# Routing of the first expert: where the weight splits, the row pieces and the count update are issued

## The chip, the cores and the metric

One core of a Trainium2 chip. The metric is the device time of one execution in microseconds (us), lower is better. Engines by the profile's names: PE (TensorE, matrix multiply), PEld (its weight loads), DVE (VectorE), ACT (ScalarE), POOL (GpSimd), SP (SyncE, which issues most transfers).

## The reference, cut to what matters

Three blocks follow each other: block-causal attention (4 x 8 heads, 576 positions, 64 wide), a mixture of eight experts, and a bilinear layer. All tensors are float32. The routing of the middle block is a greedy one with capacities:

```python
logits = x @ w_gate                      # 2304 tokens, 8 experts
order = np.argsort(-logits.flatten())
for idx in order:                        # best (token, expert) pairs first
    tok, e = idx // E, idx % E
    if assigned[tok] >= 0 or counts[e] >= cap: continue      # cap = 288
    assigned[tok] = e; counts[e] += 1
for e in range(E):
    out[mask_e] = relu(x[mask_e] @ w1[e]) @ w2[e]
# then, on its rows: ((x @ w_a) * (x @ w_b)) @ w_out
```

## The kernel before, in words

**Stages.** `attention` leaves the 2304 output rows transposed in `xT` and the logits in `logits`. Then `moe` serves the eight experts in the order in which they fill up. For each expert o: `route(o)` finds which expert fills next and which 288 tokens it takes; `ffn(o)` computes both layers of that expert and the bilinear layer of its rows; `outs(o)` scatters the result. `route(o+1)` is interleaved into `ffn(o)`, so only `route(0)` runs with no matrix work beside it.

**Order of the work.** Every engine executes its own instructions in the order in which the Python code emits them (`manual_schedule`). The functions are generators: a `yield` is a place where the caller may emit something else. For `route(0)` the caller (L756) emits nothing between the yields, apart from `pump(3)` once the tokens are known (L757), so the engine queues hold exactly the order of the source.

**route(0).** `search` (L415) finds the threshold in six digits (`QUICK`: 4, 5, 6, 6, 6 and 5 bits). For each digit, DVE compares 18 columns of tokens with 2 to the bits thresholds (L432, tile `mk`); PE counts them with 18 small matmuls (L438); DVE compares the counts with the capacity (L441, `hit`); one matmul picks the digit (L444); DVE forms the next thresholds (L449 to L454). `members` (L465) then ranks the tokens with two prefix matmuls (L490, L491) and turns the ranks into row numbers with one-hot tiles (L511) and 18 matmuls (L515); three indirect transfers on POOL (L526) fetch the 288 rows, 96 each, from the DRAM tensor `xs`. `update` (L530) lowers the capacities and marks the tokens as taken; it holds one matmul of its own (L545). `xprep` (L559) scales the fetched rows (L564, tile `xo`), transposes them (L569) and splits them into a high and a low part (L571 `xh`, L572 `xl`).

**Two fillers are emitted inside route(0).** `xrows` (L355), called `xr`, writes the 18 pieces of 128 rows into `xs`: four PE transposes (L360), an ACT copy (L362), a small POOL copy (L363) and a transfer on SP (L364) for each piece. After the last piece it closes the pool of `xT` and allocates `wbh` and `wbl` in its place. `wsplit` (L370), called `ws`, splits the 24 pieces of the bilinear weights `wa` and `wb`: a load on SP two pieces ahead (L377), an ACT cast (L384, `wah`), a DVE subtraction (L385, `wal`). Its first call issues three loads, the next ones one each.

Three row pieces are emitted ahead of `route(0)`. Each digit then emits one weight split (L439) between the counting matmuls and `hit`, and 3, 3, 3, 3, 2 and 1 row pieces behind the matmul that picks the digit (L446). In `ffn(0)` the main loop emits one more split at every eighth step (L764). Each step of `ffn` holds three matmuls of 288 columns (L635 to L637).

**Expert weights.** `pump` (L601) keeps four loads (`raw`, L610 to L614) and up to six split pieces (`spl`: ACT cast L621, DVE subtraction L622) ahead of PE. `pump(3)` starts as soon as `members(0)` is through: four loads on SP and three splits. SP also reads the expert's number from memory (L485) before it can issue these loads.

Of the kernel before, what the change touches and what calls it, by code (L numbers as in the profile page):

```python
# [338 lines left out]
def moe(ctx, tc, k, xs, rows, room, logits, w1, w2, wa, wb, wor, out, idf):  # L339
# [3 lines left out]
    E,CAP,C,R,Q=k.E,k.CAP,k.C,k.R,k.Q; F=1024; DM=512; FF=1536; XW=DM+8  # L343
# [45 lines left out]
    def bc(a,n): return a[:,:,None].to_broadcast([128,a.shape[1],n])  # L389
    def bm(a,n): return a[:,None,:].to_broadcast([128,n,a.shape[1]])  # L390

    def wait(n):
        for _ in range(n): yield
# [3 lines left out]
    xr,ws=xrows(),wsplit()  # L397
# [17 lines left out]
    def search(DIG):  # L415


        ND=len(DIG)
        quick=DIG is k.QUICK
        mk=rt.tile([128,C,TM],BF,name="mk"); hit=rt.tile([TM,E],BF,name="hit"); th=rt.tile([128,TM],I32,name="th")  # L420
        dg=rt.tile([128,1],I32,name="dg"); dgf=rt.tile([128,1],F32,name="dgf")
        bmi=rt.tile([128,1],I32,name="bmi"); bmj=rt.tile([128,TM],I32,name="bmj")
        w=rt.tile([128,E],F32,name="w"); wd=rt.tile([128,E],F32,name="wd"); wm=rt.tile([128,1],F32,name="wm"); st['w']=w
        def prepare(i):

            if i: V.tensor_tensor(bmi,bmi,dg,op=ALU.bitwise_xor)
            if i+2<ND: V.scalar_tensor_tensor(bmj,pi,DIG[i+2][0],bmi.to_broadcast([128,TM]),op0=ALU.logical_shift_left,op1=ALU.bitwise_xor)
        for i,(sh,nb) in enumerate(DIG):
            T=1<<nb
            t=(th if i else th0)[:,0:T].bitcast(F32)  # L430
            for c,n in CUT[T]:
                V.tensor_tensor(mk[:,c:c+n,0:T],bc(m[:,c:c+n],T),t[:,None,:].to_broadcast([128,n,T]),op=ALU.is_ge)  # L432
                yield from wait(3)
            if i: prepare(i-1)
            yield from wait(4)
            p=ps.tile([128,512],F32,name="m",bufs=1)
            for c in range(C):
                nc.tensor.matmul(p[0:T,0:E],mk[:,c,0:T],ca[:,0,c,:],start=c==0,stop=c==C-1)  # L438
            if quick: next(ws)  # L439
            yield from wait(1)  # L440
            V.tensor_tensor(hit[0:T],p[0:T,0:E],kk[0:T],op=ALU.is_ge)  # L441
            yield from wait(3)
            p=ps.tile([128,512],F32,name="m",bufs=1)
            nc.tensor.matmul(p[:,0:E],pw[0:T,k.SH.index(sh),:],hit[0:T],start=True,stop=True)  # L444
            if quick:
                for _ in range((3,3,3,3,2,1)[i]): next(xr)  # L446
            yield from wait(3)
            if i<ND-1:
                V.tensor_reduce(dg,p[:,0:E],axis=AX.X,op=ALU.max)  # L449
                if i==0:  # L450
                    V.tensor_scalar(bmi,dg,28,None,op0=ALU.logical_shift_left)
                    flip(bmi,dg,bmi)
                    V.scalar_tensor_tensor(th,pi,DIG[1][0],bmi.to_broadcast([128,TM]),op0=ALU.logical_shift_left,op1=ALU.bitwise_xor)
                else: V.tensor_tensor(th,bmj,dg.to_broadcast([128,TM]),op=ALU.bitwise_xor)  # L454
            else:

                V.scalar_tensor_tensor(wd,e8,1.0/16,p[:,0:E],op0=ALU.mult,op1=ALU.add)
                V.tensor_reduce(dgf,p[:,0:E],axis=AX.X,op=ALU.max)
                V.tensor_reduce(wm,wd,axis=AX.X,op=ALU.max)
                V.tensor_scalar(dg,dgf,-1.0,None,op0=ALU.add)  # L460
                V.tensor_scalar(w,wd,wm,None,op0=ALU.is_equal)
                V.tensor_tensor(bmi,bmi,dg,op=ALU.bitwise_xor)
        st['v']=bmi.bitcast(F32)

    def members(o):  # L465

        w=st['w']
        eid=rt.tile([128,1],I32,name="eid",bufs=2)
        x=rt.tile([128,2,C,E],BF,name="x4"); cw=rt.tile([128,2,C],F32,name="cw"); bt=rt.tile([128,2,C],BF,name="bt")
        V.tensor_tensor(x,ca,w[:,None,None,:].to_broadcast([128,2,C,E]),op=ALU.mult)  # L470
        V.tensor_reduce(cw,x,axis=AX.X,op=ALU.add)
        we=rt.tile([128,E],F32,name="we"); ef=rt.tile([128,1],F32,name="ef")
        if o<E-1:
            v=st['v']
            g=rt.tile([128,C],F32,name="g")
            V.scalar_tensor_tensor(g,m,v,cw[:,0],op0=ALU.is_gt,op1=ALU.mult)
            V.scalar_tensor_tensor(bt[:,1],m,v,cw[:,0],op0=ALU.is_equal,op1=ALU.mult)
            V.tensor_tensor(bt[:,0],g,cw[:,1],op=ALU.add)
        else:
            V.memset(bt[:,1],0.0)  # L480
            V.tensor_tensor(bt[:,0],un,cw[:,1],op=ALU.add)
        V.tensor_tensor(we,w,e8,op=ALU.mult)
        V.tensor_reduce(ef,we,axis=AX.X,op=ALU.add)
        V.tensor_scalar(eid,ef,-1.0,float(E),op0=ALU.mult,op1=ALU.add)
        reg=nc.sync.value_load(eid[0:1,0:1],min_val=0,max_val=E-1)  # L485
        st['reg',o]=reg
        yield from wait(7 if o<E-1 else 20)
        b2=bt.rearrange("p a c -> p (a c)")
        p=ps.tile([128,512],F32,name="m",bufs=1)
        nc.tensor.matmul(p[:,0:2*C],ub,b2,start=True,stop=True)  # L490
        nc.tensor.matmul(p[:,2*C:4*C],ones,b2,start=True,stop=True)  # L491
        yield

        pf=rt.tile([128,2*C],F32,name="pf"); z=rt.tile([128,2,C],F32,name="z"); zz=rt.tile([128,C],F32,name="zz")
        V.tensor_tensor_scan(pf,onec,p[:,2*C:4*C],1.0,op0=ALU.mult,op1=ALU.add)
        V.tensor_tensor(pf,pf,p[:,0:2*C],op=ALU.add)
        V.tensor_tensor(z.rearrange("p a c -> p (a c)"),pf,b2,op=ALU.mult)
        V.scalar_tensor_tensor(zz,z[:,0],-1.0,z[:,1],op0=ALU.add,op1=ALU.add)
        st['z']=z
        q=rt.tile([128,C,Q+1],F32,name="q"); sb=rt.tile([128,C],BF,name="sb")  # L500
        oh=rt.tile([128,C,TM],BF,name="mk")[:,:,0:R]; tq=rt.tile([128,C,Q+1,2],BF,name="tq")
        s=rt.tile([128,C],F32,name="sl")
        V.tensor_tensor(q,bc(zz,Q+1),bm(q4,C),op=ALU.is_ge)
        V.scalar_tensor_tensor(s,q[:,:,1],-float(R),zz,op0=ALU.mult,op1=ALU.add)
        V.scalar_tensor_tensor(sb,q[:,:,2],-float(R),s,op0=ALU.mult,op1=ALU.add)
        V.tensor_tensor(tq,q[:,:,:,None].to_broadcast([128,C,Q+1,2]),tok[:,:,None,:].to_broadcast([128,C,Q+1,2]),op=ALU.mult)
        yield
        p=ps.tile([128,512],F32,name="m",bufs=1)
        h=C//2
        for c0 in (0,h):  # L510
            V.tensor_tensor(oh[:,c0:c0+h],bm(r96,h),bc(sb[:,c0:c0+h],R),op=ALU.is_equal)  # L511
            yield from wait(4)
        yield from wait(4)
        for c in range(C):
            nc.tensor.matmul(p[0:R,0:2*Q+2],oh[:,c,:],tq[:,c].rearrange("p q t -> p (q t)"),start=c==0,stop=c==C-1)  # L515
        yield

        ix=rt.tile([R,Q+1,2],F32,name="ixf"); li=rt.tile([R,Q+1],F32,name="li"); idx=rt.tile([R,Q],I32,name="idx",bufs=3)
        V.tensor_copy(ix,p[0:R,0:2*Q+2].rearrange("p (q t) -> p q t",t=2))
        V.scalar_tensor_tensor(li,ix[:,:,0],128.0,ix[:,:,1],op0=ALU.mult,op1=ALU.add)  # L520
        V.tensor_tensor(idx,li[:,0:Q],li[:,1:Q+1],op=ALU.subtract)
        st['idx',o]=idx
        for _ in xr: pass
        xg=wk.tile([R,Q,XW],F32,name="xo",bufs=1)
        for q_ in range(Q):
            nc.gpsimd.indirect_dma_start(out=xg[:,q_,:],out_offset=None,in_=xs,  # L526
                                         in_offset=bass.IndirectOffsetOnAxis(ap=idx[:,q_:q_+1],axis=0))
        st['xg',o]=xg
# [47 lines left out]
    def route(o):  # L576
        if o<E-1:
            if o:
                yield from choose()
                yield from wait(1)  # L580
            yield from search(k.FEW if o else k.QUICK)
        else: last()
        yield from members(o)
        st['ready']=o
        if o<E-1: yield from update(o)
        yield from wait(8)
        while st.get('hdone',-1)<o-1: yield
        yield from xprep(o)


    D1,D2=2,2
# [168 lines left out]
    for o in range(E):  # L760
        side=route(o+1) if o+1<E else iter(())
        for i,_ in enumerate(ffn(o)):
            tick()
            if ws and i%8==0:  # L764
                if next(ws,1)==1: ws=None
            if tail is not None and next(tail,1)==1: tail=None
            if i>=SIDE: next(side,None)
            pump()
        for _ in side: pass
        tail=outs(o)  # L770
# [85 lines left out]
```

## Time and profile before

| | |
|---|---|
| median of 3 runs | 1023.86 us (1021.78 to 1024.03) |
| the profiled execution | 1020.96 us |
| its span in the profile | 1019.2 us |
| PE busy | 955.7 us (94%) |
| DVE busy | 712.0 us (70%) |
| ACT busy | 440.1 us (43%) |
| POOL busy | 204.5 us (20%) |
| mean granted clock of PE | 0.969 of full speed |

The profiled execution took 1.8 us more than its span, which runs from the first to the last instruction. All positions in the trace are microseconds from the start of the span. In the timeline a row gives the start, the length, the engine, the source line, the operation, output and inputs with shapes, the number of merged instructions, and in brackets the idle time of the engine before it with what ended it. "SPq" is SP's issue of a transfer.

### The profile page before, as it was taken

How to read it: one execution, taken by the hardware profiler on the slowest of the kernel's cores; microseconds unless marked ns; L12 is line 12 of the kernel's file. 1: busy time of each engine (PE TensorE's matmuls, PEld its weight loads, DVE VectorE, ACT ScalarE, POOL GpSimd, SP SyncE). 2: the span in 40 equal slices, each digit the busy share in tenths (PEclk: the TensorE clock that was granted, in tenths of full speed). 3: DMA queues.
4: the chain of work that ended last, by engine and by line, in shares of the span. 5: the costliest groups of instructions: out<-in, count | busy, mean ns of one | idle time of the engine just before them, and what ended most of it. 6: DMA issues, size and time to landing. Idle time of an engine off the chain costs nothing.

```text
span 1019.2 us, 20479 instructions
## 1 busy us (share of the span) xinstructions
PE 955.7 (94%) x7741; PEld 894.9 (88%) x7741; DVE 712.0 (70%) x1627; ACT 440.1 (43%) x1108; POOL 204.5 (20%) x215
## 2 busy tenths in 40 slices
PE   6998999986489999999999999999999999999996
PEld 5776877764389999999999999999999999999996
DVE  6899899984677877677667667766766776535421
ACT  5775767753354335224422522442253235224321
POOL 8676566621100011002001100200110011101001
PEclk9999999997589999999999999999999999999998
DMA  6696777624665146115403520450253046215300
GB/s 140 186 244 180 211 213 218 182 95 161 204 195 162 43 118 188 32 43 165 110 22 98 178 63 24 136 158 22 80 159 90 12 118 188 66 52 158 84 12 24
DMA packets 134563, 123.14 MB, mean 121 GB/s; under 512 B 64320, under 2 KB 97088, under 8 KB 134464
## 3 DMA queue, kind: packets, MB, share of 16 engines
q1 hardware_dynamic: 131392, 112.32, 38.9%
q0 software_dynamic: 3072, 9.51, 2.9%
q8 instruction: 61, 1.00, 0.4%
q14 instruction: 38, 0.31, 0.1%
HBM read 102.85 MB, written 18.95 MB: 120 GB/s over the span
## 4 chain that ended last, share of the span: by engine, by line
PE 79%; DVE 9%; DMA 4%; ACT 3%; POOL 3%; issue 2%; SPq 0%; ACTq 0%; DVEq 0%; POOLq 0%
PE h L635 13%; PE h L636 12%; PE h L637 12%; PE acc L635 8%; PE acc L636 8%; PE acc L637 8%; PE tr L172 3%; PE pv L190 3%; PE s L149 3%; DMA xo<-xs,idx 2%; PE m L438 1%; PE pv L149 1%; DVE mx L150 1%; PE acc L360 1%; PE h L744 1%
## 5 line engine op out<-in xcount | busy, mean ns | idle before, releaser
L635 PE MATMUL acc<-th,spl 128*128 128x288 f32 x640 | 191.7, 300 | 0.2 <-ACT th L686 0.2
L636 PE MATMUL acc<-tl,spl 128*128 128x288 f32 x640 | 189.4, 296 | 0.3
L637 PE MATMUL acc<-th,spl 128*128 128x288 f32 x640 | 189.5, 296 | 0.0
L622 DVE TENSOR_TENSOR spl<-raw,spl 128x512 fp32r<-128x512 f32 x224 | 152.9, 689 | 26.5 <-ACT spl L621 20.4
L621 ACT CAST spl<-raw 128x512 fp32r<-128x512 f32 x224 | 137.3, 620 | 37.0 <-PE acc L637 27.7
L526 POOL DMA_INDIRECT xo<-xs,idx x24 | 25.4, 1060 | 496.1 <-DVE cg L535 445.5
L636 PEld LDWEIGHTS acc<-tl,spl 128*128 128x128 f32 x640 | 120.8, 189 | 1.1 <-DVE tl L687 1.1
L635 PEld LDWEIGHTS acc<-th,spl 128*128 128x128 f32 x640 | 120.6, 188 | 0.4 <-ACT th L686 0.4
L637 PEld LDWEIGHTS acc<-th,spl 128*128 128x128 f32 x640 | 120.5, 188 | 0.0
L686 ACT CAST th<-h 128x288 fp32r<-128x288 f32 x96 | 38.3, 399 | 182.6 <-DVE h L684 180.0
L635 PE MATMUL h<-y,wah 128*128 128x288 f32 x384 | 116.2, 303 | 0.0
L635 PE MATMUL h<-y,wbh 128*128 128x288 f32 x384 | 115.2, 300 | 0.0
L636 PE MATMUL h<-y,wbh 128*128 128x288 f32 x384 | 113.4, 295 | 0.0
L637 PE MATMUL h<-y,wal 128*128 128x288 f32 x384 | 113.2, 295 | 0.0
L636 PE MATMUL h<-y,wah 128*128 128x288 f32 x384 | 113.1, 295 | 0.0
L637 PE MATMUL h<-y,wbl 128*128 128x288 f32 x384 | 113.1, 294 | 0.0
L684 DVE TENSOR_TENSOR h<-h,ta 128x288 f32<-128x288 f32 x96 | 44.5, 464 | 90.0 <-PE h L637 87.9
L679 ACT COPY ta<-h 128x288 f32<-128x288 f32 x96 | 38.3, 399 | 157.6 <-PE h L637 156.7
L635 PE MATMUL h<-xh,spl 128*128 128x288 f32 x256 | 79.5, 311 | 4.0 <-ACT xh L571 4.0
L157 ACT ACTIVATE A<-s,mx 128x128 f32<-128x128 f32 (+7 forms) x128 | 64.0, 504 | 38.3 <-DVE mx L150 36.8
L636 PE MATMUL h<-xl,spl 128*128 128x288 f32 x256 | 76.8, 300 | 1.2 <-DVE xl L572 1.2
L637 PE MATMUL h<-xh,spl 128*128 128x288 f32 x256 | 76.5, 299 | 0.0
(213 smaller groups left out, 2189.1 us busy)
## 6 DMA issues: line engine op xcount, KB each, us to landing
raw<-in_moe_w_dram SPq DMA_DIRECT2D x128, 256.0 KB, 3.2
raw<-wo SPq DMA_DIRECT2D x96, 256.0 KB, 2.7
cw<-in_moe_w_a_dram SPq DMA_DIRECT2D x12, 512.0 KB, 3.9
cw<-in_moe_w_b_dram SPq DMA_DIRECT2D x12, 512.0 KB, 4.7
cw<-in_moe_w_out_dram SPq DMA_DIRECT2D x12, 512.0 KB
xs<-spl SPq DMA_DIRECT2D x18, 260.0 KB, 2.2
kr<-in_k_dram SPq DMA_DIRECT2D x32, 128.0 KB, 5.4
qr<-in_q_dram SPq DMA_DIRECT2D x32, 128.0 KB, 2.8
```

Source lines behind the costliest of these rows:

```text
L149: nc.tensor.matmul(o,ww[:,i,:],kk[:,c:c+w],start=s0,stop=s1)
L157: nc.scalar.activation(o,view,AF.Exp,bias=mx[:,i:i+1],accum_out=sm[:,i:i+1])
L172: nc.tensor.transpose(p[:,128*m:128*m+128],A[:,off[i]+j,:],idf)
L190: nc.tensor.matmul(p[64*h:64*h+64,c,a-cut[c]:e-cut[c]],vv[:,j,h,:],AT[:,h,o:o+e-a],start=(j==0), stop=(j==(2 if c==0 else 4)),skip_group_c ...
L621: nc.scalar.copy(t[:,0,:],src)
L622: V.tensor_tensor(t[:,1,:],src,t[:,0,:].bitcast(F32),op=ALU.subtract)
L635: nc.tensor.matmul(p,wh,xh,start=s0,stop=False)
L636: nc.tensor.matmul(p,wh,xl,start=False,stop=False)
L637: nc.tensor.matmul(p,wl,xh,start=False,stop=s1)
L679: nc.scalar.copy(t,pa[:,:CAP])
L684: V.tensor_tensor(g,g,t,op=ALU.mult)
L686: later(1,lambda: nc.scalar.copy(gh,g))
```

## The change

- The digits of the first search emit no weight split any more.
- Each of the six digits emits two row pieces, where it was 3, 3, 3, 3, 2 and 1. The three pieces that are left, and the end of `xrows`, are emitted in `members`, behind the prefix matmuls and ahead of the one-hot tiles.
- For the first expert `update` is emitted behind `xprep`, no longer between the indirect transfers and `xprep`. Two weight splits are emitted where it stood.
- In `ffn(0)` a weight split is emitted at every seventh step, where it was every eighth. So 22 of the 24 splits lie there, where it was 18.

```diff
             for c in range(C):
                 nc.tensor.matmul(p[0:T,0:E],mk[:,c,0:T],ca[:,0,c,:],start=c==0,stop=c==C-1)
-            if quick: next(ws)
             yield from wait(1)
             V.tensor_tensor(hit[0:T],p[0:T,0:E],kk[0:T],op=ALU.is_ge)
...
             if quick:
-                for _ in range((3,3,3,3,2,1)[i]): next(xr)
+                for _ in range(2): next(xr)
...
         nc.tensor.matmul(p[:,2*C:4*C],ones,b2,start=True,stop=True)
+        for _ in xr: pass
         yield
...
         st['idx',o]=idx
-        for _ in xr: pass
         xg=wk.tile([R,Q,XW],F32,name="xo",bufs=1)
...
         yield from members(o)
         st['ready']=o
-        if o<E-1: yield from update(o)
+        if 0<o<E-1: yield from update(o)
+        if o==0:
+            for _ in range(2): next(ws)
         yield from wait(8)
         while st.get('hdone',-1)<o-1: yield
         yield from xprep(o)
+        if o==0: yield from update(o)
...
             tick()
-            if ws and i%8==0:
+            if ws and i%7==0:
                 if next(ws,1)==1: ws=None
```

## Rows read from the trace of the kernel before

**Rows 1.** Busy time by stretch: from:to, length, engines' busy (instructions), PE clock, DMA share, GB/s

```profile
236.60:266.00 29.40, 17.70 (x172) 15.38 (x170) 15.02 (x44) 12.39 (x23) 3.05 (x13) 0.60 0.63 215
266.00:285.10 19.10, 6.16 (x38) 4.48 (x37) 13.37 (x48) 3.91 (x8) 3.28 (x3) 0.50 0.60 174
325.00:350.00 25.00, 23.51 (x218) 22.93 (x218) 19.64 (x43) 9.72 (x21) 0.00 (x0) 1.00 0.20 64
350.00:1019.00 669.00, 655.45 (x5381) 645.40 (x5380) 427.55 (x1027) 235.04 (x520) 54.20 (x69) 1.00 0.32 91
```

**Rows 2.** What DVE waited for, 236 to 286: us in total, times, longest

```profile
DVE wal L385 <- ACT wah L384: 12.5, 6, 5.0
```

**Rows 3.** Timeline of the search, DVE and PE

```profile
236.61 0.46 DVE L432 TENSOR_TENSOR mk<-mm,mth 128x288 bf16<-128x288 f32 x1
...
242.91 0.16 PE L444 MATMUL m<-hit,mpw 16*128 16x8 bf16 x1 [5.18 <-DVE hit L441]
...
244.27 0.76 DVE L432 TENSOR_TENSOR mk<-mm,th 128x576 bf16<-128x576 f32 x1
...
247.93 1.68 PE L360 MATMUL acc<-idf,xT 128*128 128x128 f32 x12
...
256.75 0.16 PE L444 MATMUL m<-hit,mpw 64*128 64x8 bf16 x1 [1.06 <-DVE hit L441]
...
256.85 2.82 PE L360 MATMUL acc<-idf,xT 128*128 128x128 f32 x12
...
257.48 1.43 DVE L432 TENSOR_TENSOR mk<-mm,th 128x768 bf16<-128x768 f32 x2
...
259.60 1.12 PE L438 MATMUL m<-mca,mk 128*64 128x8 bf16 x18
...
261.88 1.97 PE L360 MATMUL acc<-idf,xT 128*128 128x128 f32 x8
...
263.78 0.65 PE L438 MATMUL m<-mca,mk 128*32 128x8 bf16 x18
...
265.96 0.16 PE L444 MATMUL m<-hit,mpw 32*128 32x8 bf16 x1 [1.54 <-DVE hit L441]
```

**Rows 4.** Timeline from the ranks to the fetched rows

```profile
270.07 1.58 SPq L610 DMA_DIRECT2D raw<-in_moe_w_dram  x3
...
271.48 1.86 PE L515 MATMUL m<-tq,mk 128*96 128x8 bf16 x18 [2.93 <-DVE mk L511]
...
273.01 0.62 ACT L621 CAST spl<-raw 128x512 fp32r<-128x512 f32 x1 [5.09 <-DMA raw<-in_moe_w_dram]
...
274.21 1.20 POOL L526 DMA_INDIRECT xo<-xs,idx  x1 [16.98 <-DVE g L534]
...
275.15 0.62 ACT L621 CAST spl<-raw 128x512 fp32r<-128x512 f32 x1 [0.63 <-DMA raw<-in_moe_w_dram]
...
277.19 0.92 POOL L526 DMA_INDIRECT xo<-xs,idx  x1 [0.30 <-issue]
...
282.91 0.69 DVE L564 TENSOR_TENSOR xo<-xo 96x512 f32<-96x512 f32 x1 [2.10 <-DMA xo<-xs,idx]
```

**Rows 5.** Line L364, the row writes: time from issue to landing

```profile
DMA to landing us min/median/max: 2.1/2.2/2.3
```

**Rows 6.** Line L526, all eight experts' fetches: time from issue to landing

```profile
DMA to landing us min/median/max: 4.6/4.8/5.7
```

**Rows 7.** The page's group of the expert weights' subtractions

```profile
L622 DVE TENSOR_TENSOR spl<-raw,spl 128x512 fp32r<-128x512 f32 x224 | 152.9, 689 | 26.5 <-ACT spl L621 20.4
```

**Rows 8.** Timeline: the update's head, and the first matmuls of ffn(0)

```profile
274.10 0.31 DVE L535 TENSOR_TENSOR cg<-mca,g 128x144 bf16<-128x144 bf16 x1
...
274.47 0.30 PE L545 MATMUL m<-cg,mones 128*128 128x144 bf16 x1 [1.13 <-DVE cg L535]
...
285.10 0.56 DVE L572 TENSOR_TENSOR xl<-h,xh 128x384 fp32r<-128x384 f32 x1 [0.57 <-ACT xh L571]
...
285.71 0.61 PE L636 MATMUL h<-xl,spl 128*128 128x288 f32 x1
```

## The prediction, made before the changed kernel was run

> **What bounds the kernel now.** I cut the span into stages first. From 350 us on PE is busy 655 of 669 us, so PE sets the pace and work on other engines is nearly free. The search (236.6 to 266.0) and the fetch of the rows (266.0 to 285.1) are different: PE is busy 17.7 of 29.4 us and 6.2 of 19.1 us, and the granted clock is 0.60 and 0.50 [rows 1]. These 48.5 us are a chain of dependent steps with no matrix work beside it. Whatever is taken off that chain comes off the end, since all later PE work stands behind it.
>
> Then I asked what the chain waits for. In it DVE waited 12.5 us, six times, for the ACT cast of a weight split, at the subtraction L385 [rows 2]. That subtraction is queued ahead of `hit`, the answer that every digit needs. So each of the six digits ends by its split, not by its counting. The longest wait, 5.0 us, is the first one, where the weights still had to be loaded.
>
> **Part 1, the search without splits.** I rebuild each digit from its rows. A digit starts with the matmul L444 that picks the digit before. In the trace the digit before the last starts at 256.75; its 12 transposes run 256.85 to 259.67, its comparison `mk` 257.48 to 258.91, its 18 counting matmuls start at 259.60 and take 1.12; but the next L444 comes only with the last digit, whose first transposes are at 261.88, so near 261.79 [rows 3]. Counting was through at 260.72; the missing microsecond is the split.
>
> Without the split the end is: counting, then 0.04 to `hit`, then 0.20 (`hit` itself and the step to PE) to the next L444; both small steps are estimates. With two pieces there are eight transposes, 1.97 at 261.88 where it was 2.82 for twelve [rows 3]. At this low clock:
> - First digit: `mk` ends at 237.07, 18 counts take 0.65 (as at 263.78), so L444 comes at 237.97 where it was 242.91. Saved 4.94.
> - Second digit: `mk` (244.27 + 0.76) ends 2.12 after its L444 at 242.91; plus 0.05, 0.61 for counts, 0.04 and 0.20 it lasts 3.02.
> - Three digits of 64 thresholds: the eight transposes end 2.0 after L444, counts start at about 1.95, plus 1.12, 0.04 and 0.20: 3.31 each.
> - Last digit: transposes end at 2.0, counts 0.65, so 2.88.
>
> The last L444 comes at 237.97 + 3.02 + 3 x 3.31 + 2.88 = 253.80 where it was 265.96 [rows 3]. **Saved: 12.16 us.** At the full clock (twelve transposes in 1.68 at 247.93 [rows 3]) the comparisons would be last: 3.10 three times and 2.42, so 252.7 and 13.25 saved. [...] Below this the rows give nothing.
>
> **Part 2, three pieces beside the one-hot tiles.** I keep the old positions here. PE stands idle 2.93 us ahead of the one-hot matmuls at 271.48, thus from 268.55 [rows 4]. Twelve transposes take 2.82 [rows 3]: they just fit, cost 0, and would cost up to that 0.1 to 0.3 if they began late. The last copy on ACT then ends near 272.0 and its row write lands 2.2 later [rows 5], at 274.25. The first fetch started at 274.21 [rows 4] and must wait for all rows: 0.05, between 0 and 0.5.
>
> **Part 3, splits and loads ahead of the fetch.** SP used to issue the expert weights' loads at 270.07. Now three row writes and four loads of the two splits stand ahead of them on SP, so the first load of that burst goes out at about 272.4. Unloaded, the first of three landed 2.94 after its issue (cast at 273.01) and the third 2.14 later (275.15): 1.07 each [rows 4]. The third expert piece is the seventh of the new burst: 272.4 + 2.94 + 6 x 1.07 = 281.8. Its cast takes 0.62 [rows 4], its subtraction 0.69 [rows 7], and all three scalings of the fetched rows (0.69 each) stand behind it on DVE: they end near 285.3. Before, the last scaling ended at 283.60, held by the third fetch [rows 4]. Cost 1.7, and 0.4 because the three transposes then come at once: 2.1, for the burst is nearest to the three loads of before. The bounds are 0 (the fetch stays last) and 3.3 (a pitch a fifth longer, as the fetch shares the engines). The two splits' own DVE and ACT work hides in the wait for the loads.
>
> The fetch's third transfer took 5.7 us, where the median over all experts is 4.8 [rows 6], beside four loads on SP. [...]
>
> **Part 4, `update` behind `xprep`.** Where it stood, DVE was waiting for the fetch anyway, so removing it gains 0 (it gave cover, not time). Where it goes, its matmul L545 stands in PE's queue ahead of the first matmul of `ffn(0)` and waits for `cg`. The last subtraction `xl` ends at 285.66; then a small operation of about 0.23 and `cg` of 0.31, then L545 of 0.30 [rows 8]. The second matmul of `ffn(0)`, which needs `xl`, used to start at 285.71 [rows 8]; it now follows L545 and the first one, at about 286.7, but no longer with a gap behind it. Cost 0.8, between 0.4 and 1.4. The rest of the update, some 2 us on DVE, delays the next expert splits, of which three are in hand, 36 matmuls or over 4 us of PE work (218 took under 25 us [rows 1]): 0.
>
> **Part 5, 22 splits in `ffn(0)`.** Four more subtractions are 2.8 us of DVE. Between 325 and 350 DVE is busy 19.6 of 25 us and PE still 23.5 [rows 1]; what PE misses there, 1.5 us, can grow with a busier DVE. I take 0.5, between 0 and 2.8 (all of it exposed). All splits are still issued before the columns that need them: the last at step 147, needed from step 156.
>
> **Sum.** -12.2 + 0.05 + 2.1 + 0.8 + 0.5 = -8.8, with a little for a partly full clock: **-9.0 us**. On the profiled execution (1020.96, span 1019.2) this gives 1012.0. The median of the runs is 2.9 above that execution, so on the median: 1023.86 - 9.0 = **1014.9**.
>
> **Rivals.**
> *The search runs at the full clock.* For it: without waits for the split PE is busy about 3.0 of each 3.3 us. Against it: the clock stayed at 0.50 to 0.60 here with PE more than half busy [rows 1]. Price: 1.1 more saved, and the last pieces land earlier, which takes 1 to 1.5 off Part 3: -11.5, thus 1012.4. [...]
> *The burst holds the fetch itself.* Last row writes, eight loads and the fetch meet; the fetch itself lands 4 us late and Part 3 costs 6 instead of 2.1: saved only 5, thus 1019. For it: 5.7 against 4.8 [rows 6]. [...]
> *The row pieces pace the search, not the splits.* Then DVE's wait would pass to PE's transposes, and nothing much is saved: 1023. Against it: at 256.75 counting was through 1 us ahead of `hit` even with twelve transposes [rows 3].
> [...]
>
> **How the numbers follow.** About 0.2% (2 us) is what a measurement of this kernel can tell from no change. Chances: the forecast 0.66, full clock 0.15, burst 0.12, row pieces 0.04, slower 0.03. The range takes in the first three: the low end is the full clock with Parts 4 and 5 at their least, -13, thus 1011.0; the high end has Part 3 at 3.3, Part 4 at 1.4 and Part 5 at 2.0: -5.4, thus 1018.5. Faster 0.94, no change 0.03, slower 0.03.
>
> **What would show it.** The waits of DVE should no longer have L385 behind ACT in the search; the first L444 should stand near 238.0 and the last near 253.8. Ahead of the last scaling DVE should wait for an expert load, not for the fetch, and L545 should stand directly ahead of the first matmul of `ffn(0)`, whose second one should start near 276.6 where it was 285.71. From there to the end the length should be that of before, within 1 us. I am wrong if a digit still lasts over 4 us, if the fetch's last transfer takes over 7 us, or if PE idles more than 3 us in `ffn(0)`.

## The result, and the profile after

The changed kernel took 1013.26 us (median of 5 runs, 1010.71 to 1014.97), the kernel before 1023.86 beside it: a ratio of 0.990, 95% interval 0.9878 to 0.9921, so 8 to 12.5 us less. The forecast was 1014.9, 9.0 less. The profiled execution of the changed kernel took 1013.26 us, its span 1011.5.

Busy time by stretch, columns as in [rows 1]: the search, from its first comparison to the last matmul that picks a digit, and the way from there to the first matmul of `ffn(0)`.

```profile
235.45:252.88 17.43, 14.54 (x156) 12.39 (x154) 11.37 (x38) 6.76 (x13) 4.62 (x13) 0.62 0.46 171
252.88:274.73 21.85, 7.62 (x54) 6.54 (x54) 13.97 (x41) 8.53 (x16) 3.47 (x3) 0.58 0.84 257
```

The search is 11.9 us shorter (29.35 before, from 236.61 to 265.96 [rows 3]). The stretch behind it is 2.7 us longer (19.16 before, 265.96 to 285.12), and PE's clock in the search is hardly higher. What DVE waited for from 236 to 277 (us, times, longest) shows what took the place of [rows 2]:

```profile
DVE hit L440 <- PE m L438: 4.2, 6, 1.1
DVE spl L624 <- ACT spl L623: 2.8, 3, 2.1
DVE wal L385 <- ACT wah L384: 2.6, 2, 2.4
...
DVE xo L563 <- DMA xo<-xs,idx: 0.7, 1, 0.7
```

Each `hit` now waits for the counting, and for nothing else. The timeline of the search answers to [rows 3]; two of the digits stand for all:

```profile
235.45 0.46 DVE L432 TENSOR_TENSOR mk<-mm,mth 128x288 bf16<-128x288 f32 x1
...
236.88 0.16 PE L443 MATMUL m<-hit,mpw 16*128 16x8 bf16 x1 [0.32 <-DVE hit L440]
...
246.63 0.16 PE L443 MATMUL m<-hit,mpw 64*128 64x8 bf16 x1 [0.25 <-DVE hit L440]
246.72 1.97 PE L360 MATMUL acc<-idf,xT 128*128 128x128 f32 x8
...
248.62 1.12 PE L438 MATMUL m<-mca,mk 128*64 128x8 bf16 x18
...
249.78 0.16 DVE L440 TENSOR_TENSOR hit<-m,mkk 64x8 bf16<-64x8 f32 x1 [0.60 <-PE m L438]
250.00 0.16 PE L443 MATMUL m<-hit,mpw 64*128 64x8 bf16 x1 [0.25 <-DVE hit L440]
...
252.88 0.16 PE L443 MATMUL m<-hit,mpw 32*128 32x8 bf16 x1 [0.24 <-DVE hit L440]
```

A digit of 64 thresholds lasts 3.37 us (246.63 to 250.00): eight transposes, then the counts, then `hit`. From the row numbers to the first matmuls of `ffn(0)`, answering to [rows 4, 8], the timeline reads:

```profile
258.93 2.08 SPq L377 DMA_DIRECT2D wraw<-wa  x4
...
260.36 0.16 DVE L521 TENSOR_TENSOR idx<-li 96x3 int32<-96x3 f32 x1
...
262.47 1.13 POOL L525 DMA_INDIRECT xo<-xs,idx  x1 [10.55 <-DMA wraw<-wa]
...
268.75 0.69 DVE L624 TENSOR_TENSOR spl<-raw,spl 128x512 fp32r<-128x512 f32 x1 [0.45 <-ACT spl L623]
...
270.11 1.96 DVE L563 TENSOR_TENSOR xo<-xo 96x512 f32<-96x512 f32 x3 [0.67 <-DMA xo<-xs,idx]
...
274.69 0.30 PE L544 MATMUL m<-cg,mones 128*128 128x144 bf16 x1 [1.65 <-DVE cg L534]
...
275.12 0.44 PE L638 MATMUL h<-xl,spl 128*128 128x288 f32 x1
```

The fetch starts 1.95 us behind the row numbers (260.52 to 262.47); in the kernel before it was 0.29. DVE is through with the third expert piece at 269.44 and then still waits 0.67 for the fetched rows. The update's matmul stands ahead of `ffn(0)` as forecast.

The last difference lies in `ffn(0)`. From its second matmul (285.71 before [rows 8], 275.12 after) to the first scatter transpose it takes 94.7 us before and 97.2 after. The start of that transpose is the first of the two positions in these groups of the scatter's line (min/median/max ns, first and last start), before and after:

```profile
L744 PE MATMUL h<-idf,y x96: 270/272/316, 380.4 to 1010.5; 128*96 128x128 f32 x96
```

```profile
L746 PE MATMUL h<-idf,y x96: 270/272/312, 372.3 to 1002.8; 128*96 128x128 f32 x96
```

Below, "search" is the first stretch, "scalings" the end of the third scaling counted from the end of `idx`, and "`ffn(0)`" this last length. For one execution each:

| | search | fetch starts | scalings | `ffn(0)` | ratio to the kernel before (95%) |
|---|---|---|---|---|---|
| before | 29.35 | 0.29 | 9.68 | 94.7 | 1 |
| changed | 17.43 | 1.95 | 11.55 | 97.2 | 0.990 (0.9878 to 0.9921) |
| a1, splits back | 27.02 | 1.71 | 11.24 | 94.8 | 1.0001 (0.9980 to 1.0022) |
| a2, pieces back | 15.28 | 0.29 | 8.83 | 96.4 | 0.9877 (0.9854 to 0.9900) |
| a3, update back | 16.60 | 1.71 | 15.29 | 96.9 | 0.9950 (0.9928 to 0.9972) |
| a4, splits behind the rows | 16.62 | 1.70 | 10.54 | 95.5 | 0.9922 (0.9893 to 0.9951) |
| b1, more transposes | 15.27 | 1.42 | 10.55 | 96.8 | 0.9886 (0.9859 to 0.9913) |
| b2, pieces back, update in the fetch | 15.28 | 0.30 | 8.28 | 97.2 | 0.9877 (0.9849 to 0.9905) |
| b3, pieces back, other steps | 15.27 | 0.29 | 8.74 | 97.4 | 0.9895 (0.9869 to 0.9921) |
| b4, b2 and b3 | 15.27 | 0.29 | 8.24 | 96.3 | 0.9874 (0.9843 to 0.9904) |
| c1, the change again | 17.18 | 1.71 | 12.13 | 96.2 | 0.9915 (0.9894 to 0.9936) |
| c2, subtractions on POOL | 17.42 | 1.96 | 11.74 | 97.9 | 0.9933 (0.9913 to 0.9952) |
| c3, b2 and c2 | 15.29 | 0.29 | 8.44 | 98.0 | 0.9876 (0.9856 to 0.9897) |
| d1, four splits early | 15.27 | 0.29 | 14.50 | 95.2 | 0.9912 (0.9880 to 0.9944) |

The attention ahead of all this is the same code everywhere, and yet the search began between 233.8 and 242.0 us in these executions. Whole times are therefore only good to some 3 us; the lengths in the table are what the experiments are read by.

### The profile page after: what moved, and what is told of

Read it like the earlier page. It is cut to its first block, busy times and chain, and to the rows that moved or that the text cites. A ratio compares the mean times of both kernels' runs of the same rounds, so it can differ in the third digit from the quotient of the medians.

```text
span 1011.5 us, 20472 instructions
## 1 busy us (share of the span) xinstructions
PE 954.3 (94%) x7741; PEld 893.9 (88%) x7741; DVE 711.2 (70%) x1627; ACT 439.9 (43%) x1108; POOL 206.4 (20%) x215
## 4 chain that ended last, share of the span: by engine, by line
PE 80%; DVE 10%; DMA 5%; ACT 2%; issue 2%; POOL 1%; SPq 0%; POOLq 0%; DVEq 0%; ACTq 0%
PE h L637 13%; PE h L638 12%; PE h L639 12%; PE acc L638 8%; PE acc L637 8%; PE acc L639 8%; PE tr L172 4%; PE s L149 3%; PE pv L190 3%; DMA xo<-xs,idx 3%; PE m L438 2%; DVE mx L150 1%; PE pv L149 1%; PE h L746 1%; DVE cf L801 1%
## 5 line engine op out<-in xcount | busy, mean ns | idle before, releaser
L624 DVE TENSOR_TENSOR spl<-raw,spl 128x512 fp32r<-128x512 f32 x224 | 153.0, 689 | 29.3 <-ACT spl L623 23.3
L686 DVE TENSOR_TENSOR h<-h,ta 128x288 f32<-128x288 f32 x96 | 44.4, 463 | 87.9 <-PE h L639 85.9
```

The source lines that it names most:

```text
L624: V.tensor_tensor(t[:,1,:],src,t[:,0,:].bitcast(F32),op=ALU.subtract)
L686: V.tensor_tensor(g,g,t,op=ALU.mult)
```

## The experiments

**a1: the splits back in the digits.**

```diff
+            if quick: next(ws)
             yield from wait(1)
...
-        if o==0:
-            for _ in range(2): next(ws)
...
-            if ws and i%7==0:
+            if ws and i%8==0:
```

> The changed kernel with the splits back in the six digits (one each), none beside the fetch, and every eighth step in ffn(0); the pieces stay two per digit, update stays behind xprep. If the splits paced the search: each digit ends by a split again, the search (first comparison to last digit-picking matmul, 17.4 us in the changed kernel, 29.4 before) comes back to about 27, a little under before because only two copies stand ahead of the cast; the fetch starts 0.3 us behind the row numbers again, and time is about 1013.3 + 9.8 - 1.9 (fetch) - 2 (ffn(0)) = 1019. If the row pieces paced it: the search stays under 20 us and time stays within 2 us of 1013.3.

Measured: a search of 27.02 us and the time of the kernel before. The splits were the cause; pieces and update alone win nothing. One part of the expectation failed: the fetch still started 1.71 us late, with no split's load near it (a4 shows why). DVE's waits show the splits again:

```profile
DVE wal L385 <- ACT wah L384: 10.2, 6, 5.1
```

**a2: the row pieces back in the digits.**

```diff
-                for _ in range(2): next(xr)
+                for _ in range((3,3,3,3,2,1)[i]): next(xr)
...
-        for _ in xr: pass
         yield
...
         st['idx',o]=idx
+        for _ in xr: pass
```

> The changed kernel with the pieces as before (3, 3, 3, 3, 2, 1 per digit, none beside the one-hot tiles). If the transposes end last in a digit at the low clock: the search grows by 0.85 us in each of three digits and 0.75 in the second, from 17.4 to 20.7. If the late row writes held the fetch (it started 1.95 us behind the row numbers, 0.29 before): it starts 0.3 us behind them again and ends 1.9 earlier, so 1013.3 + 3.3 - 1.9 = 1014.7. If the loads of the two splits held it by themselves: it still starts over 1.5 us late and time is about 1016.6.

Measured: the opposite of the first part. With half as many transposes again in a digit, the search is 2.15 us shorter than the changed kernel's, because PE ran it at the full clock, a granted 1.00 where it was 0.62. Its row by stretch, clock in the third column from the end:

```profile
236.66:251.94 15.28, 12.10 (x172) 10.26 (x170) 11.38 (x38) 8.41 (x17) 4.08 (x13) 1.00 0.71 264
```

Its digits of 64 thresholds take 2.81 us. The second part came: with the rows written early the fetch starts 0.29 behind `idx`, although the loads of the two splits are still there.

**b1: more work for PE, and nothing else.** In the changed kernel, four transposes of the identity behind the two pieces of each digit:

```diff
                 for _ in range(2): next(xr)
+                pj=ps.tile([128,512],F32,name="acc",bufs=4)
+                for g in range(4): nc.tensor.transpose(pj[:,128*g:128*g+128],idf,idf)
```

> The changed kernel with four more PE transposes per digit behind the two pieces, of the identity into a bank that nobody reads, so twelve per digit as with three pieces. If PE's clock decides the digit (the changed kernel had a granted clock of 0.62 in its search and 3.36 us per 64-threshold digit, the run with three pieces 1.00 and 2.81): the clock stays at 1.00, the digits take 2.81 and the search 15.3 us where it was 17.4; time falls by about 2. If the number of transposes decides: the clock stays low, digits take 4.2 and the search about 20. If it was the extra copies or row writes of three pieces: nothing changes, 17.4 or a little more.

Measured: a search of 15.27 us, with the same two copies and two row writes per digit as the changed kernel.

```profile
234.67:249.94 15.27, 12.47 (x175) 10.68 (x174) 11.37 (x38) 6.37 (x13) 4.60 (x13) 1.00 0.52 194
```

So the clock made the difference between eight and twelve transposes, not the rows. All seven kernels with twelve transposes in most digits and no split there had a granted clock of 1.00 in the search and took 15.3 us. Twelve alone are not enough: the kernel before had them too, in digits of 3.9 to 5.0 us, at 0.60 [rows 1]. With eight, the same search code ran at 0.62 in the changed kernel and at 0.77 and 0.76 in a3 and a4, where it took 16.6 us.

**a4: the two early splits behind the fetched rows.**

```diff
-        if o==0:
-            for _ in range(2): next(ws)
         yield from wait(8)
         while st.get('hdone',-1)<o-1: yield
         yield from xprep(o)
-        if o==0: yield from update(o)
+        if o==0:
+            for _ in range(2): next(ws)
+            yield from update(o)
```

> The changed kernel with its two early splits, and their four loads, emitted behind xprep instead of ahead of the fetch. If those loads held the last row write and the fetch: it starts at most 0.8 us behind the row numbers, its transfers land in 4.8 to 5.7 us (7.6, 6.7 and 5.7 in the changed kernel), and time falls by 1.5 to 2 to about 1011.5. If the last row writes are late by themselves, or any load behind them does the same: the fetch still starts over 1.5 us late, and time stays at 1013.3.

Measured: the fetch still starts 1.70 us late, but its transfers land in 5.3 us, where they took 5.7 to 7.6 in the changed kernel, and the scalings end 1.0 earlier. So the loads of the splits slowed the transfers, and did not hold the start. What does is seen in POOL's records of its waits (ns min/median/max, first and last start), of the kernel before, of the changed one and of a4:

```profile
L526 POOLq EVENT_SEMAPHORE  x6: 17/43/83627, 270.1 to 282.9; - x6
```

```profile
L525 POOLq EVENT_SEMAPHORE  x6: 17/43/86234, 261.3 to 271.4; - x6
L525 POOL DMA_INDIRECT xo<-xs,idx x3: 921/1134/1412, 262.5 to 265.6; - x3
```

```profile
L525 POOLq EVENT_SEMAPHORE  x6: 17/43/86724, 266.8 to 276.1; - x6
L525 POOL DMA_INDIRECT xo<-xs,idx x3: 921/1070/1137, 268.0 to 270.8; - x3
```

The first record marks the end of the wait for the last row write; the longest, of 84 to 87 us, is the last one, which waits for the next expert. In the changed kernel the last row write is issued at 258.48 and lands 2.8 us later, at 261.3, and the first transfer starts 1.1 us behind that (262.5). It is the same 1.1 in a4 (266.8 and 268.0) and in b1 (258.2 and 259.3). In the kernel before the wait was over at 270.1, long before `idx` was ready at 273.92, and only 0.29 was left. What the 1.1 us consist of, these runs do not show.

**a3: update back in the fetch.**

```diff
-        if 0<o<E-1: yield from update(o)
+        if o<E-1: yield from update(o)
...
-        if o==0: yield from update(o)
```

> The changed kernel with update back between the fetch and xprep, two splits behind it. If its move cost what its place in PE's queue says: the second matmul of ffn(0) starts 0.05 us behind the last subtraction xl again (0.98 in the changed kernel), and time falls by 0.8 to about 1012.5. If DVE's 2.6 us of update ahead of the fetched rows delay the scalings: the gain is used up or more, 1013.3 or above.

Measured: slower than the change, scalings at 15.29 us. But this is not the price of update. Its `yield`s let `pump` issue three more loads ahead of the splits' loads on SP:

```profile
259.06 1.58 SPq L611 DMA_DIRECT2D raw<-in_moe_w_dram  x3
260.84 0.36 SPq L615 DMA_DIRECT2D raw<-in_moe_w_dram  x1
263.53 0.37 SPq L611 DMA_DIRECT2D raw<-in_moe_w_dram  x1
265.04 0.34 SPq L615 DMA_DIRECT2D raw<-in_moe_w_dram  x1
266.14 0.37 SPq L611 DMA_DIRECT2D raw<-in_moe_w_dram  x1
266.56 6.73 SPq L377 DMA_DIRECT2D wraw<-wa  x5
```

Each of the three waits for a buffer (DVE is through with the three pieces ahead at 263.50, 265.01 and 266.11), and the splits' loads (258.93 in the changed kernel) stand behind them at 266.56. DVE then waits for the split, with the scalings behind it. The run tells nothing on update; b2 asks again.

**b2: update whole, right behind the transfers, with the pieces of a2.**

```diff
         if o==0:
+            for _ in update(o): pass
             for _ in range(2): next(ws)
...
-        if o==0: yield from update(o)
```

> The run with three pieces per digit, and update emitted whole right behind the indirect transfers, ahead of the two splits (the run with update back had the splits' loads behind loads that wait for free buffers, and its scalings ended 15.3 us behind the row numbers). If update costs only by its place in PE's queue: the scalings end about 8.8 us behind the row numbers as with three pieces alone, the second matmul of ffn(0) starts 0.05 to 0.1 behind the last xl instead of 0.98, and 0.8 is saved against three pieces alone: 0.9870 of the kernel before. If DVE has no room for it in the fetch: the scalings end over 9.6 behind the row numbers and nothing is saved.

Measured: scalings at 8.28 us, not later than in a2, and the second matmul of `ffn(0)` follows `xl` again:

```profile
271.01 0.56 DVE L571 TENSOR_TENSOR xl<-h,xh 128x384 fp32r<-128x384 f32 x1 [0.23 <-ACT xh L570]
...
271.63 0.61 PE L638 MATMUL h<-xl,spl 128*128 128x288 f32 x1
```

From the first comparison to this matmul a2 takes 35.1 us and b2 33.6: the place of update is worth 1 us and the earlier scalings the rest. The ratio cannot show it, since `ffn(0)` was 0.8 longer in this execution.

**b3 and b4: other steps for the splits in `ffn(0)`.**

```diff
-            if ws and i%7==0:
+            if ws and (i%7==0 if i<44 else i%20 in (5,12,15)):
```

> The run with three pieces per digit, with the 22 splits of ffn(0) at every seventh step only up to step 44 and then at steps 5, 12 and 15 of every 20 (a digit of the next routing has 20 steps; its count is compared at step 11 of 20). If PE's longer waits in ffn(0) (3.3 us on hit, mk and th, 1.5 before) come from splits queued on DVE just ahead of that comparison: these waits fall under 1.5 us and the stretch from the second matmul of ffn(0) to its first scatter transpose falls by 1.5 to 2 from 96.4 us. If they come from DVE's load of 22 splits: they stay within 0.5 of 3.3.

> Three pieces per digit, update whole behind the transfers, and the new steps in ffn(0), together. If the three effects are separate: 2.5 to 3 us under three pieces alone, about 0.985 of the kernel before. If they overlap: within 1 us of it.

Measured: a miss. PE's waits in `ffn(0)` (us, times, longest) in the kernel before, the changed one, and b3:

```profile
PE m L444 <- DVE hit L441: 0.9, 1, 0.9
PE m L438 <- DVE mk L432: 0.6, 1, 0.6
```

```profile
PE m L443 <- DVE hit L440: 2.5, 2, 1.5
...
PE m L438 <- DVE mk L432: 0.5, 1, 0.5
PE acc L637 <- ACT th L688: 0.3, 1, 0.3
```

```profile
PE m L443 <- DVE hit L440: 1.1, 2, 0.9
PE m L438 <- DVE mk L432: 1.1, 2, 0.6
PE h L638 <- DVE y L674: 0.9, 1, 0.9
```

The waits moved to other instructions and kept their sum (3.1 us, against 3.3 in the changed kernel and 3.1 in a2), and the stretch stayed at 97.4. It is not where the 22 splits stand. With 18 at every eighth step (a1) waits and stretch are those of before. b4, at 0.9874, is within 1 us of a2 (0.9877), so its three effects did not show as separate ones in the time.

**d1: four early splits, 20 at every eighth step**, on top of b2.

```diff
-            for _ in range(2): next(ws)
+            for _ in range(4): next(ws)
...
-            if ws and i%7==0:
+            if ws and i%8==0:
```

> Three pieces per digit, update whole behind the transfers, four splits instead of two ahead of the fetched rows, and so 20 splits in ffn(0) at every eighth step. If the number and step of the splits in ffn(0) make PE wait there: its waits on hit, mk and th go back from 3.3 us to about 1.5, as with 18 splits at every eighth step, and the stretch from the second matmul to the first scatter transpose to about 95 (96.3 to 97.4 with 22). If they come from the moved pieces or the earlier start of the stretch: 96 or more. Two more splits ahead of the fetched rows cost nothing where DVE only waits for the fetch, up to 1.4 us if it does not: scalings end 8.3 to 9.7 us behind the row numbers. Time 0.986 of the kernel before.

Measured: `ffn(0)` goes back to 95.2 us, with waits of 2.3 on `hit` and `mk`. Not all of that comes from the splits. `ffn(0)` by stretch, columns as in [rows 1], of the kernel before, the changed one, b2 and d1:

```profile
285.71:380.37 94.66, 92.28 (x755) 90.44 (x755) 74.68 (x176) 41.36 (x88) 2.85 (x4) 0.98 0.45 132
```

```profile
275.12:372.27 97.15, 92.93 (x755) 90.78 (x755) 78.34 (x188) 42.52 (x90) 2.85 (x4) 0.97 0.46 140
```

```profile
271.63:368.81 97.18, 93.20 (x756) 91.08 (x756) 77.29 (x180) 43.44 (x92) 2.85 (x4) 0.97 0.47 140
```

```profile
275.52:370.69 95.17, 92.11 (x755) 89.96 (x755) 75.75 (x178) 42.33 (x90) 2.86 (x4) 0.98 0.46 137
```

The length less PE's busy time is what PE idles: 2.4, 4.2, 4.0 and 3.1 us. With 18 splits it is 2.4 and 2.5 (a1), with 20 3.1, with 22 from 3.6 to 4.7: more splits go with more waiting. But of the 2.0 us between b2 and d1 only 0.9 are waits. PE was also busy 1.1 us less, and its granted clock in the first 6 us of the stretch was 0.73 in d1 and 0.52 in b2. That start differs from one execution to the next: 0.55 in the changed kernel, 0.70 in c1, which is the same kernel. So the number of splits is the likely cause of the waits, and the clock at the start the likely cause of much of the rest.

The time is a miss (0.9912, 0.986 expected), since the scalings end at 14.50: SP issued six loads from 254.53 to 262.78, since only four buffers hold them (the fifth went out at 261.86, when the first was split), and the expert weights' loads came behind, at 262.99.

```profile
254.53 8.25 SPq L377 DMA_DIRECT2D wraw<-wa  x6
262.99 1.57 SPq L612 DMA_DIRECT2D raw<-in_moe_w_dram  x3
```

**c1, c2 and c3: the subtractions on POOL.** c1 is the changed kernel again, c2 the changed kernel with the edit below, c3 the kernel of b2 with it.

```diff
-            V.tensor_tensor(l[:,d,s],r,h[:,d,s].bitcast(F32),op=ALU.subtract)
+            (V if i<2 else nc.gpsimd).tensor_tensor(l[:,d,s],r,h[:,d,s].bitcast(F32),op=ALU.subtract)
```

> The changed kernel itself once more, beside the two below and the kernel before on one chip: 0.990 of the kernel before, search 16.6 to 17.4 us, and the stretch of ffn(0) from its second matmul to the first scatter transpose 96.5 to 97.2 us (94.7 in the kernel before).

> The changed kernel with the subtractions of the 22 splits in ffn(0) on POOL, which is idle there, instead of DVE. If DVE's load of 22 splits makes PE wait in ffn(0): PE's waits on hit, mk and th fall from 3.3 us to under 1.5, the stretch of ffn(0) falls from 96.5 to 97.2 to 95 or less, and time falls by about 2. If they come from something else in the stretch (loads, the update's place, the clock at its start): the stretch stays at 96 to 97.5.

> Three pieces per digit, update whole behind the transfers, and the 22 subtractions on POOL. If the effects add up: 2 us from the search at the full clock, 1.9 from the fetch, 0.8 from update and 2 from ffn(0) against the changed kernel, so about 0.984 of the kernel before. If POOL's subtractions slow DVE or delay wb's columns: not better than 0.9875.

Measured: a miss. `ffn(0)` did not shrink (97.9 and 98.0). DVE was rid of 22 subtractions and was not freer (busy 78.1 us of this stretch in c1, 79.9 in c2), for its other work became longer. Groups of DVE from 280 to 350 (busy us, mean ns) in c1, then in c2:

```profile
L624 DVE TENSOR_TENSOR spl<-raw,spl 128x512 fp32r<-128x512 f32 x20 | 13.7, 686 | 0.2
...
L686 DVE TENSOR_TENSOR h<-h,ta 128x288 f32<-128x288 f32 x9 | 4.2, 461 | 0.6 <-PE h L639 0.6
...
L427 DVE SCALAR_TENSOR_TENSOR bmj<-mpi,bmi 128x128 int32<-128x128 int32 x3 | 0.9, 289 | 0.1
```

```profile
L624 DVE TENSOR_TENSOR spl<-raw,spl 128x512 fp32r<-128x512 f32 x22 | 20.5, 941 | 4.7 <-ACT spl L623 4.5
...
L686 DVE TENSOR_TENSOR h<-h,ta 128x288 f32<-128x288 f32 x8 | 3.7, 463 | 3.0 <-PE h L639 3.0
L427 DVE SCALAR_TENSOR_TENSOR bmj<-mpi,bmi 128x128 int32<-128x128 int32 x3 | 3.0, 998 | 0.1
```

So c2 could not free DVE and does not settle what makes PE wait. c1 gave 0.9915 on this chip, c3 0.9876.

**The best version.** Every kernel with three pieces per digit and two early splits lies at 0.987 to 0.990, b4 lowest with 0.9874, c3 with the narrowest interval. On one chip c3 took 1008.46 us where the change took 1012.16. Every one of the five executions of c3 (up to 1009.04) lies below every one of the six of the change (from 1010.44), so that c3 is faster is shown, by about 3.7 us on that chip; the intervals of the two ratios touch (0.9897 and 0.9894), as both hold the scatter of the kernel before. By the lengths in the table it is 2.1 us of search and 2.7 to 3.3 up to the scalings, less what `ffn(0)` and 0.3 ahead of `idx` give back. Which of the versions with three pieces is best is not shown. Counted from the first comparison to the end, which leaves the attention out, b2 takes 769.7 us, b4 770.2, c3 771.1, b3 771.2 and a2 772.5, one execution each, where the change takes 776.1 and 776.3 and the kernel before 782.6.

## Why the prediction was right, and where its steps were not

**Part 1 held.** Forecast 12.16 saved, measured 29.35 - 17.43 = 11.92. The first digit took 1.43 us where 1.36 was forecast; the others came out at 3.02, 3.36, 3.37, 3.37 and 2.88 us where 3.02, three times 3.31 and 2.88 stood. In the digits of 64 thresholds the counts start 1.99 us behind the picking matmul, not 1.95, and `hit` with the step to PE takes 0.22, not 0.20.

**Part 2 was mis-sized.** The transposes did fit ahead of the one-hot matmuls, and the row numbers even came 0.32 earlier. The last row write landed 8.4 us behind the last digit, as forecast (8.3). But the cost was put at 0.05, at most 0.5, and it was 1.66: the prediction let the fetch start as soon as the rows were there, and POOL took 1.1 us more between that wait and its first transfer. In the trace of before this step was hidden, as the rows were there 3.8 us ahead of `idx`.

**Part 3 had the wrong last event.** I expected the third expert load to hold the scalings; it was through at 269.44, and the fetch came last. The sum of Parts 2 and 3 up to the scalings was right by this exchange: 1.75 forecast, 11.55 - 9.68 = 1.87 measured. The 0.4 for the transposes did not come. The rival that the burst holds the fetch was nearer to what happened, at a smaller price than its 6 us. The fetch, on its own queue, landed behind the burst all the same: its first transfer at 270.1, 0.3 behind the eighth load (issued at 262.97, landed 6.9 later), and in b1 and b2 by 0.1 and 0.4. How the two queues shared the transfers, no run shows.

**Part 4 held**: the second matmul starts 0.98 behind the last `xl` instead of 0.05, the third 0.76 later than it did, 0.8 forecast. Its sentence that the old place was free is also borne out by b2.

**Part 5 was mis-sized**: 0.5 forecast, with a bound of 2.8, and 2.5 measured in the changed kernel; over the runs with 22 splits the stretch was 95.5 to 98.0 against 94.7 and 94.8 with 18. PE's waits on `hit`, `mk` and `th` grew from 1.5 to 3.3 us, its whole idle time by 1.8; the other 0.7 is a longer busy time, at a lower clock in the first 6 us (0.55, 0.63 before). One of the signs that the prediction named for itself did occur here: PE idles 4.2 us in `ffn(0)`, over the 3 that it set. So did another: from the second matmul to the end it is 2.9 us longer than before, not within 1. That the load of DVE makes PE wait fits a1 and d1, c2 could not test it, and it is not shown.

**The sum.** From the first comparison to the end the profiled executions differ by 782.59 - 776.05 = 6.54 us, and c1 gives 776.3 again. The medians differ by 10.6, and in the second measurement by 8.6 (6.5 to 10.8 by its interval). The forecast of 9.0 lies between. The 6.5 are 11.9 of search and 0.3 up to `idx` saved, and 1.9 up to the scalings, 0.9 up to the second matmul, 2.5 in `ffn(0)` and 0.4 behind it lost. So Parts 2 to 5 cost over 5 us where 3.45 was put, and that the median came out within 2 us of the forecast is in part luck. No run shows the 0.2 that the sum takes for a partly full clock: the search ran at a granted clock of 0.62 and saved 11.9, not 12.2. What the medians have beyond the 6.5 isn't located by any stage; the scatter of the attention ahead, 8 us over these executions, hides it. That remains open. The low end of the forecast's range has a slip as well: -13 needs Part 3 at 0; with what the rival of the full clock takes off it, the sum is about -12.

**The rival of the full clock** was real, but not for this change: with two pieces per digit and no split there the search ran at a granted clock of 0.62 to 0.77, with three at 1.00, and that two pieces instead of three could cost something was not among the cases. Its price was too small: at the full clock the digits of 64 thresholds took 2.81 us, not 3.10, and the search saved 14.1, where 13.25 was the bound. The twelve transposes of 1.68 us at 247.93, which Part 1 took for the full clock, had a granted clock of 0.87; at 1.00 they took 1.53 (a2). And its argument that the clock stayed at 0.50 to 0.60 with PE more than half busy holds for the search only; at 0.50 PE was busy 6.2 of 19.1 us [rows 1]. More work on PE raised it in b1, where nothing but four useless transposes per digit took the granted clock from 0.62 to 1.00.

## What to carry to other kernels

Filler work on a chain of dependent steps cost here what it put in an engine's queue ahead of the next step, so look at what stands directly ahead of the answer: one split per digit cost 10.2 us of DVE's waits (a1), while twelve transposes per digit cost less than eight, by the clock (a search of 15.3 us at 1.00, and of 17.4 at 0.62). Moving the filler moved its price: late rows started the fetch 1.95 us behind the row numbers instead of 0.29, early loads blocked SP's queue as soon as they needed a buffer that was not free (8.25 us for six loads in d1), and a DVE with 22 splits instead of 18 went with 4.2 us of idle PE in `ffn(0)` instead of 2.4. Size each new place by what is queued behind it, not by its own length.

## What the runs showed of the hardware that I had not expected

- More PE work made a latency-bound stretch shorter: with no split in the digits, eight transposes per digit ran at a granted clock of 0.62 to 0.77 and a search of 16.6 to 17.4 us, twelve at 1.00 and 15.3 us.
- The first indirect transfer started 1.1 us behind the end of POOL's wait for the DRAM writes (the changed kernel, a4 and b1), and 0.29 behind the indices where that wait was long over (by 3.8 us, in the kernel before).
- The subtractions moved to POOL slowed DVE by more than they took off it: its busy time in `ffn(0)` was 78.1 us with them and 79.9 without. DVE's subtraction L624 went from 686 to 941 ns and L427 from 289 to 998, while L686 stayed at 461 and 463. What sets those two apart from L686, no run shows.
